# Sinkhorn attention and a bilinear FFN on one core: mixing k and v with tokens on partitions, up to three units ahead

## The chip, the cores and the metric

The kernel runs on one core of a Trainium2 chip. The metric is the device time of one execution in microseconds (us). "PE" is TensorE, "DVE" VectorE, "ACT" ScalarE, "POOL" GpSimd and "SP" SyncE, which here only issues DMAs.

## The reference, cut to what matters

```python
# batch 4, heads 8, sequence 768, head_dim 64; the sequence is cut into 8 blocks of 96
P = sort_net                                    # 8 x 8 for each head
for _ in range(5):                              # Sinkhorn: exp, then rows, then columns
    ...
k_sorted = einsum('bhij,bhjcd->bhicd', P, k_b)  # "mix": blocks of k weighted by P
v_sorted = einsum('bhij,bhjcd->bhicd', P, v_b)
scores   = q_b @ k_sorted.T / sqrt(64)          # 96 x 96 in each block
attn_out = softmax(scores) @ v_sorted
x        = attn_out as (3072, 512)
out      = ((x @ w_a) * (x @ w_b)) @ w_out      # 512 -> 1536 -> 512
```

## The kernel before

Heads are taken in pairs: four pairs make a batch, pairs 4 to 7 are batch 1, pairs 8 to 11 batch 2, and so on. The FFN of one batch and the attention of the next are interleaved on PE: after every few FFN steps stands one unit of attention work. `c` mixes k and v of a pair, `s` computes the scores and their exponential, `o` applies the weights to v and sends the result, by a DMA transpose, into `xT`, the left operand of the next batch's FFN.

```python
def stage_mix(g, what, engines):                # the mix, with head_dim on partitions
    src2 = loaded[g][0 if what == "k" else 1]   # 128 tokens x 2 heads x 384
    to = (kTs if what == "k" else vTs)[g % NBUF]
    mix = psA.tile([P, 2, 512], FP32, tag="A", name="mix")
    for c in range(NCH):                        # 6 chunks x 2 heads = 12 matmuls,
        for e in range(2):                      # weights 128x64, 128 columns each
            nc.tensor.matmul(mix[e * D:(e + 1) * D, c // 3, c % 3 * P:(c % 3 + 1) * P],
                             lhsT=src2[:, e, c * D:(c + 1) * D],
                             rhs=s_all[:, 2 * g + e], start=True, stop=True)
    ...                                         # evict to kT (ACT) or vT (half DVE, half ACT)
    if what == "v" and g > HP:                  # v must turn back: tokens on partitions
        nc.sync.dma_start_transpose(out=vss[g % NBUF][:, :, V0:V0 + P],
                                    in_=to.rearrange("p i t -> p (i t)"))

def to_xT(g):                                   # all of the FFN's x goes this way
    nc.sync.dma_start_transpose(out=xT[:, g % HP, :]..., in_=xp...)

def ffn_ab(b, m, t):                            # "pf": 8 matmuls of 384 columns, 4 for a, 4 for b
    ...                                         # ACT evicts a, DVE multiplies it with b into hT

def store(b, c, po):                            # one of six 128x512 pieces of a batch's output
    o_sb = ffp.tile([P, DMODEL], FP32, tag="o_sb", name="o_sb", bufs=3)
    copy("act" if c % 2 == 0 else "dve", o_sb, po)
    ...                                         # DMA to the output, from the SP queue

def c_(g):                                      # a unit of the interleaved attention
    ...
    stage_mix(g, "k", ("act",))
    stage_mix(g, "v", ("dve", "act"))
    if 2 * HP - 2 <= g < B * HP - 2:            # the gate holds the loads back on POOL
        nc.gpsimd.tensor_copy(out=gate, in_=kTs[g % NBUF][0:1, 0:1])
        load_pair((g + 2) // HP, (g + 2) % HP)
# units of a batch: c0 s0 c1 s1 c2 o0 s2 c3 o1 s3 o2 o3
```

The softmax here doesn't subtract the row's maximum and nothing guards it: scores larger than these inputs give would overflow.

Of the kernel before, what the change touches and what calls it, by code (L numbers as in the profile page):

```python
# [9 lines left out]
FP32 = mybir.dt.float32  # L10
BF16 = mybir.dt.bfloat16
# [11 lines left out]
def kernel(  # L23
# [11 lines left out]
    nc = tc.nc  # L35
    P = 128
    B, H, S, D = q.shape
    NB = sort_net.shape[-1]
    BLK = S // NB
# [6 lines left out]
    NCH = S // P  # L46
    HP = H // 2
    KA = DMODEL // P
    KO = DFF // P
# [5 lines left out]
    V0 = 16  # L55
    W = NCH * D
# [8 lines left out]
    att = ctx.enter_context(tc.tile_pool(name="att", bufs=4))  # L65
    ffp = ctx.enter_context(tc.tile_pool(name="ffp", bufs=2))
    psA = ctx.enter_context(tc.tile_pool(name="psA", bufs=2, space=PSUM))
# [18 lines left out]
    loaded = {}  # L86

    def load_pair(b, hp):
        tiles = []
        for name, t in (("k2", k), ("v2", v), ("q2", q)):  # L90
            base = (b * H + 2 * hp) * S * D
            if b == 0 and name == "q2":
                continue
            to = ld.tile([P, 2, W], BF16, tag=name, name=name)
            nc.gpsimd.dma_start(out=to, in_=_ap(t, base, [[W, P], [S * D, 2], [1, W]]))  # L95
            tiles.append(to)
        loaded[b * HP + hp] = tiles
# [27 lines left out]
    NBUF = 3  # L125
    kTs = [const.tile([P, S + PAD], BF16, name=f"kT{n}") for n in range(NBUF)]
    vTs = [const.tile([P, NB, P], BF16, name=f"vT{n}") for n in range(NBUF)]
    eTs = [const.tile([BLK, 2, 2, HB + PAD], BF16, name=f"eT{n}") for n in range(NBUF)]
    vss = [const.tile([P, NB, VW], BF16, name=f"vs{n}") for n in range(NBUF)]
# [11 lines left out]
    st = {}  # L141
# [7 lines left out]
    gate = const.tile([1, 1], BF16, name="gate")  # L149
    s_all = const.tile([P, BH, NB, CG], BF16, name="s_all")  # L150
# [9 lines left out]
    def copy(eng, out, in_):  # L160
        if eng == "act":
            nc.scalar.copy(out=out, in_=in_)  # L162
        else:
            nc.vector.tensor_copy(out=out, in_=in_)  # L164
# [79 lines left out]
    def pair_q(g):  # L244
        qc = qtp.tile([P, NCH, 2, D], BF16, tag="qc", name="qc", bufs=4)
        nc.gpsimd.tensor_copy(out=qc.rearrange("p c e d -> p e c d"),  # L246
                              in_=loaded[g][2].rearrange("p e (c d) -> p e c d", c=NCH))
        st[g, "qc"] = qc

    def stage_q(g):  # L250
        qT = qtp.tile([P, NCH, P], BF16, tag="qTf", name="qTf", bufs=4)
        nc.sync.dma_start_transpose(out=qT, in_=st[g, "qc"].rearrange("p c e d -> p (c e d)"))
        st[g, "qT"] = qT

    def turn_q(g, eng="dve"):
        q2 = loaded[g][2] if g >= HP else q_first[:, 2 * g:2 * g + 2]
        q_ps = psF.tile([P, NCH, P], BF16, tag="F", name="q_ps")
        for c in range(NCH):
            for e in range(2):
                nc.tensor.matmul(q_ps[e * D:(e + 1) * D, c, :],  # L260
                                 lhsT=q2[:, e, c * D:(c + 1) * D],
                                 rhs=ident, is_transpose=True)
        qT = qtp.tile([P, NCH, P], BF16, tag="qT", name="qT")
        copy(eng, qT, q_ps)
        st[g, "qT"] = qT

    def turn_v(g):
        vT, vs = vTs[g % NBUF], vss[g % NBUF]
        vs_ps = psF.tile([P, NB, P], BF16, tag="F", name="vs_ps")
        for i in range(NB):  # L270
            nc.tensor.matmul(vs_ps[:, i], lhsT=vT[:, i], rhs=ident, is_transpose=True)
        nc.vector.tensor_copy(out=vs[0:BLK, :, V0:V0 + P], in_=vs_ps[0:BLK])

    def stage_mix(g, what, engines):
        src2 = loaded[g][0 if what == "k" else 1]
        to = (kTs if what == "k" else vTs)[g % NBUF]
        pitch, whole = (BLK, S + PAD) if what == "k" else (P, NB * P)
        mix = psA.tile([P, 2, 512], FP32, tag="A", name="mix")
        for c in range(NCH):
            for e in range(2):  # L280
                nc.tensor.matmul(  # L281
                    mix[e * D:(e + 1) * D, c // 3, c % 3 * P:(c % 3 + 1) * P],
                    lhsT=src2[:, e, c * D:(c + 1) * D],
                    rhs=s_all[:, 2 * g + e], start=True, stop=True)
        for hf, eng in enumerate(engines):
            n = 2 // len(engines)
            for u in range(n):
                d1 = _ap(to, (hf + u) * 3 * CG, [[whole, P], [CG, 3], [pitch, NB], [1, CG]])
                s1 = _ap(mix, (hf + u) * 512, [[1024, P], [P, 3], [CG, NB], [1, CG]])
                copy(eng, d1, s1)  # L290
        if what == "v" and g > HP:
            nc.sync.dma_start_transpose(out=vss[g % NBUF][:, :, V0:V0 + P],
                                        in_=to.rearrange("p i t -> p (i t)"))

    def stage_scores(g):
        kT, qT, eT = kTs[g % NBUF], st[g, "qT"], eTs[g % NBUF]
        for hf in range(2):
            sc = psA.tile([P, 2, 512], FP32, tag="A", name="sc")
            for i in range(NBH):
                for e in range(2):  # L300
                    blk = hf * NBH + i
                    nc.tensor.matmul(  # L302
                        sc[:, e, i * BLK:(i + 1) * BLK],
                        lhsT=kT[e * D:(e + 1) * D, blk * BLK:blk * BLK + P],
                        rhs=qT[e * D:(e + 1) * D, :, blk * CG:(blk + 1) * CG],
                        start=True, stop=True)
            nc.scalar.activation(out=eT[:, hf, :, 0:HB], in_=sc[0:BLK, :, 0:HB],  # L307
                                 func=AF.Exp, scale=float(scale))

    def stage_o(g):  # L310
        xp = att.tile([BLK, NB, 2, D], BF16, tag="xp", name="xp")
        for hf in range(2):
            one_o(eTs[g % NBUF], hf, vss[g % NBUF], hf * NBH, xp, NB)
        st[g, "xp"] = xp

    def to_xT(g):
        xT, xp = xT_of(g // HP), st[g, "xp"]
        nc.sync.dma_start_transpose(
            out=xT[:, g % HP, :].rearrange("p (i t) -> p i t", i=NB),
            in_=xp.rearrange("p i e d -> p (i e d)"))  # L320


    hTs = {}
# [10 lines left out]

    def hT_of(b):
        if b not in hTs:
            hTs[b] = ffp.tile([P, KO, S], BF16, tag="hT", name="hT")
        return hTs[b]

    def ffn_ab(b, m, t, begun=()):  # L340
# [58 lines left out]
    with tc.manual_schedule(engines={ET.PE, ET.Pool, ET.SP}):  # L399
        with tc.manual_schedule(engines={ET.Activation, ET.DVE}):  # L400
# [7 lines left out]
            for it in range(5):  # L408
# [15 lines left out]
                if it > 0:  # L424
                    nc.tensor.matmul(heat[0:NB, 1, 0:NB], lhsT=rsum, rhs=rsum,
                                     start=True, stop=True)
# [103 lines left out]
            us.append(lambda: half_x(1, HP - 1, "dve"))  # L530
            return us

        def units_full(b):
            g0, us = b * HP, []

            def c_(g):
                if g < 2 * HP - 2:
                    turn_q(g)
                stage_mix(g, "k", ("act",))
                stage_mix(g, "v", ("dve", "act"))  # L540
                if 2 * HP - 2 <= g < B * HP - 2:
                    nc.gpsimd.tensor_copy(out=gate, in_=kTs[g % NBUF][0:1, 0:1])  # L542
                    load_pair((g + 2) // HP, (g + 2) % HP)

            def s_(g):
                stage_scores(g)
                if g == HP:
                    turn_v(g)
                if g in (HP, HP + 1):
                    stage_q(g + 2)  # L550
                if 2 * HP <= g + 1 < B * HP:
                    pair_q(g + 1)
                    stage_q(g + 1)

            def o_(g):
                stage_o(g)
                to_xT(g)

            for u, n in ((c_, 0), (s_, 0), (c_, 1), (s_, 1), (c_, 2), (o_, 0), (s_, 2), (c_, 3),
                         (o_, 1), (s_, 3), (o_, 2), (o_, 3)):  # L560
                us.append(lambda u=u, g=g0 + n: u(g))
            return us

        def interleave(steps, units, spare, slow=0):
            n, done = len(steps), 0
# [4 lines left out]
                    units[done]()  # L570
                    done += 1

        def paced(ab, po, units, spare):
            steps = ab + po
            total = len(steps) - 2 * spare
            done = 0
            for now, step in enumerate(steps, 1):
                step()
                while done < len(units) and done * total < now * len(units):
                    units[done]()  # L580
                    done += 1

        steps = [lambda: ffn_ab(0, 0, 0, begun[0:2]), lambda: ffn_ab(0, 1, 0, begun[2:4]),
                 lambda: ffn_ab(0, 2, 0, begun[4:5])]
# [3 lines left out]
        for b in range(B):  # L588
            ab = [lambda m=m, t=t, b=b: ffn_ab(b, m, t)
                  for m in range(KO) for t in range(2) if b > 0 or t == 1]  # L590
            po = [f for c in range(NCH) for f in ffn_out(b, c)]
            paced(ab, po, units_full(b + 1) if b + 1 < B else [], 3 if b == 0 else 2)


# [28 lines left out]
```

## Time and profile before

| | before |
|---|---|
| median of 3 executions | 245.35 us (245.03 to 245.57) |
| span of the profiled execution | 243.3 us |
| PE busy | 237.4 us, 98% |
| granted PE clock | 1.00 |

The first lines to read are on the page of the profile: busy time by engine with its share of the span, and the chain of work that ended last, by engine and by line.

```profile
...
PE 237.4 (98%) x2309; PEld 141.6 (58%) x2309; DVE 109.1 (45%) x258; ACT 104.4 (43%) x204; POOL 61.4 (25%) x88
...
PE 93%; DVE 4%; ACT 1%; DMA 1%; issue 0%
PE pf L332 52%; PE po L377 24%; PE mix L281 4%; PE o_ps L231 3%; PE sc L302 2%; PE mixh L180 2%; PE po L362 1%; PE vs_ps L208 1%; PE xt_ps L222 1%; PE sc L195 1%; DMA p_nat<-in_sort_net_dram 1%; PE heat L168 1%; PE two L332 1%; PE q_ps L260
...
```

PE is busy for 98% of the span, and the chain runs over PE for 93% of it, so the time is what PE must stream. The next view is the same chain in order of time (start us, length us, what), at the mixes of pairs 5 and 7.

```profile
...
51.00 0.46 PE q_ps L260 x12
51.46 0.67 PE mix L281 x24
52.13 1.41 PE pf L332 x8
...
63.83 0.79 PE mix L281 x24
64.62 1.41 PE pf L332 x8
...
```

A pair's two mixes are 24 matmuls in 0.79 us, or 0.67 us where the q turns (`q_ps`) come first. The eight projections (`pf`) behind them take 1.41 us; eight projections in the open take 1.30 us (2.60 us for 16, elsewhere in the same view). So a pair that stands between projections costs 0.12 us at the change to the small matmuls and 0.11 us at the change back, 0.90 us in all.

```profile
...
xT<-xp SPq DMA_TRANSPOSE x2, 2.8
```

The transpose of pair 7's `xT`, the last one that batch 1's FFN needs, is the second of the two issued from 75.43 us. It lands 2.8 us after its issue, by about 80 us, 4 us before PE asks for it. POOL's line for the first load of pair 10 (start us, us) is needed for the comparison below:

```profile
...
87.45 0.72 POOL L95 DMA_DIRECT2D k<-in_k_dram  x1 [0.34 <-issue]
...
```

### The profile page before, as it was taken

Reading aid. Unit: us, or ns where it says so; the run is one execution under the profiler, and the core shown is the slowest. Engines: PE = TensorE matmul, PEld = TensorE weight load, DVE = VectorE, ACT = ScalarE, POOL = GpSimd, SP = SyncE. Lnnn points to the kernel's source line nnn. Section 1 sums busy time; section 2 is a strip of 40 time slices with the busy share of each in tenths; the row PEclk is TensorE's granted clock in tenths of the full one; section 3 lists DMA queues with packets and bytes.
Section 4 is the critical chain, followed back from the end, with each engine's and each line's share of the span. In section 5 each row is a group of like instructions: output and inputs, shape, how many; then the busy total and the mean of one; then the engine's idle time right before and its main releaser. Section 6 shows DMA issues by size and latency. Waiting matters only on the chain.

```text
span 243.3 us, 5625 instructions
## 1 busy us (share of the span) xinstructions
PE 237.4 (98%) x2309; PEld 141.6 (58%) x2309; DVE 109.1 (45%) x258; ACT 104.4 (43%) x204; POOL 61.4 (25%) x88
## 2 busy tenths in 40 slices
PE   7999999999999999999999999999999999999994
PEld 7776666666554466666654466666654466665442
DVE  6774557555435234464534144363625144344110
ACT  3675853565630175736330165737330133333001
POOL 8766569623220053240400054200000000000000
PEclk9999999999999999999999999999999999999999
DMA  5999999985999589993964369923524310000132
GB/s 78 202 198 196 196 201 201 203 138 83 158 204 153 130 70 155 171 138 70 136 115 122 115 120 114 159 51 58 47 75 131 109 43 0 3 0 1 46 129 86
DMA packets 53930, 28.04 MB, mean 115 GB/s; under 512 B 30736, under 2 KB 50960, under 8 KB 53904
## 3 DMA queue, kind: packets, MB, share of 16 engines
q0 software_dynamic: 20944, 14.16, 41.6%
q1 hardware_dynamic: 32816, 13.45, 28.0%
q8 instruction: 18, 0.29, 0.5%
q14 instruction: 8, 0.07, 0.1%
q10 hardware_dynamic: 144, 0.07, 0.1%
HBM read 28.32 MB, written 6.29 MB: 142 GB/s over the span
## 4 chain that ended last, share of the span: by engine, by line
PE 93%; DVE 4%; ACT 1%; DMA 1%; issue 0%
PE pf L332 52%; PE po L377 24%; PE mix L281 4%; PE o_ps L231 3%; PE sc L302 2%; PE mixh L180 2%; PE po L362 1%; PE vs_ps L208 1%; PE xt_ps L222 1%; PE sc L195 1%; DMA p_nat<-in_sort_net_dram 1%; PE heat L168 1%; PE two L332 1%; PE q_ps L260 1%; DVE xp L237 1%
## 5 line engine op out<-in xcount | busy, mean ns | idle before, releaser
L353 DVE TENSOR_TENSOR hT<-a_sb,pf 128x384 bf16<-128x384 bf16 x95 | 52.6, 553 | 73.8 <-PE pf L332 46.4
L332 PE MATMUL pf<-xT,w_a_sb 128*128 128x384 bf16 x380 | 78.0, 326 | 0.2 <-ACT xT L162 0.2
L332 PE MATMUL pf<-xT,w_b_sb 128*128 128x384 bf16 x380 | 77.5, 326 | 0.0
L352 ACT CAST a_sb<-pf 128x384 bf16<-128x384 f32 x95 | 45.5, 479 | 60.9 <-PE pf L332 41.3
L377 PE MATMUL po<-w_out_sb,hT 128*128 128x512 bf16 x276 | 61.9, 379 | 0.0
L332 PEld LDWEIGHTS <-w_b_sb 128*128 128x128 bf16 x384 | 37.5, 98 | 24.8 <-issue 0.3
L332 PEld LDWEIGHTS <-w_a_sb 128*128 128x128 bf16 x384 | 34.9, 98 | 22.2
L377 PEld LDWEIGHTS <-hT 128*128 128x128 bf16 x276 | 26.3, 98 | 30.0
L162 ACT COPY o_sb<-po 128x512 f32<-128x512 f32 (+1 forms) x13 | 7.5, 577 | 46.8 <-PE po L377 45.2
L164 DVE COPY o_sb<-po 128x512 f32<-128x512 f32 (+1 forms) x12 | 7.9, 656 | 35.2 <-PE po L377 26.3
L307 ACT ACTIVATE eT<-sc 96x768 bf16<-96x768 f32 x24 | 18.0, 802 | 6.9 <-PE sc L302 6.9
L542 POOL COPY gate<-kT 1x1 bf16<-1x1 bf16 x8 | 1.4, 179 | 74.7 <-ACT kT L162 74.7
L237 DVE TENSOR_TENSOR xp<-o_ps,rec 96x512 bf16<-96x512 f32 x24 | 15.9, 684 | 0.6 <-DVE rec L235 0.2
L162 ACT CAST kT<-mix 128x384 bf16<-128x384 f32 x24 | 10.3, 482 | 8.0 <-PE mix L281 8.0
L95 POOL DMA_DIRECT2D k<-in_k_dram x16 | 11.6, 724 | 4.5 <-PE pf L332 2.3
L95 POOL DMA_DIRECT2D v<-in_v_dram x16 | 11.5, 721 | 3.1 <-DMA w_b_sb<-in_moe_w_b_dram 1.2
L231 PEld LDWEIGHTS <-eT 96*128 96x128 bf16 x256 | 10.4, 97 | 3.2 <-DVE xp L237 0.6
L235 DVE RECIPROCAL rec<-o_ps 96x8 f32<-96x8 f32 x32 | 5.6, 189 | 13.8 <-PE o_ps L231 13.8
L231 PE MATMUL o_ps<-vs,eT 96*128 96x65 bf16 x256 | 11.3, 193 | 0.2 <-DVE xp L237 0.2
L246 POOL COPY qc<-q 128x768 bf16<-128x768 bf16 x10 | 8.4, 842 | 7.2 <-DMA q<-in_q_dram 7.2
L95 POOL DMA_DIRECT2D q<-in_q_dram x12 | 8.7, 721 | 1.7 <-DMA w_a_sb<-in_moe_w_a_dram 0.7
L168 PE MATMUL heat<-warm 128*128 128x128 bf16 x84 | 7.6, 264 | 1.3 <-DVE warm L77 1.3
(80 smaller groups left out, 158.3 us busy)
## 6 DMA issues: line engine op xcount, KB each, us to landing
out_dram<-o_sb SPq DMA_DIRECT2D x17, 256.0 KB, 2.0
k<-in_k_dram POOLq DMA_DIRECT2D x16, 192.0 KB, 6.0
v<-in_v_dram POOLq DMA_DIRECT2D x16, 192.0 KB, 6.4
q<-in_q_dram POOLq DMA_DIRECT2D x12, 192.0 KB, 6.7
w_a_sb<-in_moe_w_a_dram POOLq DMA_DIRECT2D x6, 256.0 KB, 9.8
w_b_sb<-in_moe_w_b_dram POOLq DMA_DIRECT2D x6, 256.0 KB, 10.0
w_out_sb<-in_moe_w_out_dram POOLq DMA_DIRECT2D x3, 512.0 KB, 10.8
out_dram<-o_sb SPq DMA_DIRECT2D x12, 128.0 KB, 2.4
```

Source lines behind the costliest of these rows:

```text
L95: nc.gpsimd.dma_start(out=to, in_=_ap(t, base, [[W, P], [S * D, 2], [1, W]]))
L162: nc.scalar.copy(out=out, in_=in_)
L168: nc.tensor.matmul(ps[:, 0:cols], lhsT=warm[:, 0:P], rhs=warm[:, 0:cols], start=True, stop=True)
L231: nc.tensor.matmul(o_ps[:, e, i * (D + 1):(i + 1) * (D + 1)], lhsT=eT[:, hf, e, i * BLK:i * BLK + P], rhs=vs[0:BLK, i0 + i, V0 - 1 + e * ( ...
L237: nc.vector.tensor_tensor(out=_ap(xp, i0 * 2 * D, [[nxp * 2 * D, BLK], [D, 2], [2 * D, NBH], [1, D]]), in0=_ap(o_ps, 1, [[1024, BLK], [511 ...
L246: nc.gpsimd.tensor_copy(out=qc.rearrange("p c e d -> p e c d"), in_=loaded[g][2].rearrange("p e (c d) -> p e c d", c=NCH))
L281: nc.tensor.matmul(mix[e * D:(e + 1) * D, c // 3, c % 3 * P:(c % 3 + 1) * P], lhsT=src2[:, e, c * D:(c + 1) * D], rhs=s_all[:, 2 * g + e], ...
L307: nc.scalar.activation(out=eT[:, hf, :, 0:HB], in_=sc[0:BLK, :, 0:HB], func=AF.Exp, scale=float(scale))
L332: nc.tensor.matmul(pf[:, 0:HW], lhsT=w_sb[:, kc, m * P:(m + 1) * P], rhs=x_cols(b, kc, t), start=(kc == 0), stop=(kc == KA - 1))
L352: nc.scalar.copy(out=a_sb, in_=pf[:, 0:HW])
L353: nc.vector.tensor_mul(out=hT[:, m, t * HW:(t + 1) * HW], in0=a_sb, in1=ab[1][:, 0:HW])
L377: nc.tensor.matmul(held["po"], lhsT=hTs[b][:, m, c * P:(c + 1) * P], rhs=w_out_sb[:, m, :], start=(m == 0), stop=(m == KO - 1))
```

## The change

The intent is to take work off PE. For k of pairs 5 to 15 and v of pairs 8 to 15 the operands of the mix are swapped: the mixing matrix becomes the weight and the tokens come out on partitions, in 2 matmuls of 384 columns instead of 12 of 128. The result then lies the wrong way round for the scores, so each such mix needs a DMA transpose from SP, and a copy on POOL that puts the tokens in block order. For v a second transpose follows, as before. To hide this the mixes run up to three units ahead: batch 2's first two pairs are now mixed in the phase of batch 0's FFN. One hT buffer is given up.

```diff
+    def stage_plain(g, what, engines):
+        mix = psA.tile([P, 2, 512], FP32, tag="A", name="mix")
+        for e in range(2):
+            nc.tensor.matmul(mix[:, e, 0:W], lhsT=s_all[:, 2 * g + e], rhs=src2[:, e], ...)
+        nat = att.tile([P, NCH, 2, D], BF16, tag="nat", name="nat")
+        ...                                                  # evict mix to nat
+        nc.sync.dma_start_transpose(out=turned, in_=nat...)
+        st[g, what] = turned
+    def in_order(g, what):
+        nc.gpsimd.tensor_copy(out=to, in_=st[g, what]...)    # turned to kT or vT
+    def return_v(g):
+        nc.sync.dma_start_transpose(out=vss[g % NBUF]..., in_=vTs[g % NBUF]...)
...
-                if 2 * HP - 2 <= g < B * HP - 2:
-                    nc.gpsimd.tensor_copy(out=gate, in_=kTs[g % NBUF][0:1, 0:1])
-                    load_pair((g + 2) // HP, (g + 2) % HP)
...
+        plan(0, "c4", "c5", "s4", "c6", "s5", "o4", "c7", "s6", "o5", "c8", "s7", "o6", "o7", "c9")
+        plan(1, "s8", "c10", "s9", "o8", "c11", "s10", "o9", "c12", "s11", "o10", "o11", "c13")
+        plan(2, "s12", "c14", "s13", "o12", "c15", "s14", "o13", "s15", "o14", "o15")
+        after = [[] for _ in seq]
+        for n, (b, u, g) in enumerate(seq):
+            if u is c_ and g > HP:
+                for what in "kv":
+                    if plain(g, what):
+                        after[n + 1].append(lambda g=g, what=what: in_order(g, what))
+                after[n + 3 if g % HP == 0 else n + 1].append(lambda g=g: load_later(g))
+                if plain(g, "v"):
+                    after[n + 2].append(lambda g=g: return_v(g))
...
-            hTs[b] = ffp.tile([P, KO, S], BF16, tag="hT", name="hT")
+            hTs[b] = ffp.tile([P, KO, S], BF16, tag="hT", name="hT", bufs=1)
```

The functions in `after[n]` run when unit n has been issued. On POOL, therefore, the loads of pair g+2 stand behind the reorder copies of pair g.

More of the change, by code (lines that the diff above doesn't have):

```diff
@@ L290, in stage_mix, with plain, stage @@
                 copy(eng, d1, s1)
-        if what == "v" and g > HP:
-            nc.sync.dma_start_transpose(out=vss[g % NBUF][:, :, V0:V0 + P],
-                                        in_=to.rearrange("p i t -> p (i t)"))
+    def plain(g, what):
+        return g >= (2 * HP if what == "v" else HP + 1)
+    def stage_plain(g, what, engines):
+        src2 = loaded[g][0 if what == "k" else 1]
+        mix = psA.tile([P, 2, 512], FP32, tag="A", name="mix")
+        for e in range(2):
+            nc.tensor.matmul(mix[:, e, 0:W], lhsT=s_all[:, 2 * g + e], rhs=src2[:, e],
+                             start=True, stop=True)
+        nat = att.tile([P, NCH, 2, D], BF16, tag="nat", name="nat")
+        step = 2 // len(engines)
+        for u, eng in enumerate(engines):
+            copy(eng, nat[:, :, u * step:(u + 1) * step].rearrange("p c e d -> p e c d"),
+                 mix[:, u * step:(u + 1) * step, 0:W].rearrange("p e (c d) -> p e c d", c=NCH))
+        turned = att.tile([P, NCH, P], BF16, tag="turned", name="turned")
+        nc.sync.dma_start_transpose(out=turned, in_=nat.rearrange("p c e d -> p (c e d)"))
+        st[g, what] = turned
+    def stage(g, what, engines):
+        (stage_plain if plain(g, what) else stage_mix)(g, what, engines)
+    def in_order(g, what):
+        if what == "k":
+            to = kTs[g % NBUF][:, 0:S].rearrange("p (i c t) -> p c i t", i=NB, c=NCH)
+        else:
+            to = vTs[g % NBUF][:, :, 0:BLK].rearrange("p i (c t) -> p c i t", c=NCH)
+        nc.gpsimd.tensor_copy(out=to, in_=st[g, what].rearrange("p c (i t) -> p c i t", i=NB))
+    def return_v(g):
+        nc.sync.dma_start_transpose(out=vss[g % NBUF][:, :, V0:V0 + P],
+                                    in_=vTs[g % NBUF].rearrange("p i t -> p (i t)"))
     def stage_scores(g):
@@ L531, in units_half, with c_ @@
             return us
-        def units_full(b):
-            g0, us = b * HP, []
-            def c_(g):
-                if g < 2 * HP - 2:
-                    turn_q(g)
-                stage_mix(g, "k", ("act",))
-                stage_mix(g, "v", ("dve", "act"))
-                if 2 * HP - 2 <= g < B * HP - 2:
-                    nc.gpsimd.tensor_copy(out=gate, in_=kTs[g % NBUF][0:1, 0:1])
-                    load_pair((g + 2) // HP, (g + 2) % HP)
-            def s_(g):
-                stage_scores(g)
-                if g == HP:
-                    turn_v(g)
-                if g in (HP, HP + 1):
-                    stage_q(g + 2)
-                if 2 * HP <= g + 1 < B * HP:
-                    pair_q(g + 1)
-                    stage_q(g + 1)
-            def o_(g):
-                stage_o(g)
-                to_xT(g)
-            for u, n in ((c_, 0), (s_, 0), (c_, 1), (s_, 1), (c_, 2), (o_, 0), (s_, 2), (c_, 3),
-                         (o_, 1), (s_, 3), (o_, 2), (o_, 3)):
-                us.append(lambda u=u, g=g0 + n: u(g))
-            return us
+        def c_(g):
+            stage(g, "k", ("act",))
+            stage(g, "v", ("dve", "act"))
+            if HP < g < 2 * HP:
+                return_v(g)
+            if g >= 2 * HP:
+                pair_q(g)
+                stage_q(g)
@@ new lines, in s_, with o_, load_later, plan @@
+        def s_(g):
+            stage_scores(g)
+            if g == HP:
+                turn_v(g)
+            if g in (HP, HP + 1):
+                stage_q(g + 2)
+        def o_(g):
+            stage_o(g)
+            to_xT(g)
+        def load_later(g):
+            if 2 * HP - 2 <= g < B * HP - 2:
+                load_pair((g + 2) // HP, (g + 2) % HP)
+        units = [[] for _ in range(B)]
+        seq = []
+        def plan(b, *names):
+            for name in names:
+                seq.append((b, {"c": c_, "s": s_, "o": o_}[name[0]], int(name[1:])))
@@ L564, in interleave, with unit @@
+        def unit(u, g, then):
+            if u is c_ and g < 2 * HP - 2:
+                turn_q(g)
+            u(g)
+            for f in then:
+                f()
+        for (b, u, g), then in zip(seq, after):
+            units[b].append(lambda u=u, g=g, then=then: unit(u, g, then))
         def interleave(steps, units, spare, slow=0):
@@ L571, in interleave, with paced @@
                     done += 1
-        def paced(ab, po, units, spare):
+        def paced(ab, po, units, spare, last):
             steps = ab + po
             total = len(steps) - 2 * spare
-            done = 0
+            main, done = len(units) - last, 0
             for now, step in enumerate(steps, 1):
                 step()
-                while done < len(units) and done * total < now * len(units):
+                while done < main and done * total < now * main:
                     units[done]()
                     done += 1
+                if now == len(steps) - 1 and last:
+                    units[main]()
         steps = [lambda: ffn_ab(0, 0, 0, begun[0:2]), lambda: ffn_ab(0, 1, 0, begun[2:4]),
@@ L591 @@
             po = [f for c in range(NCH) for f in ffn_out(b, c)]
-            paced(ab, po, units_full(b + 1) if b + 1 < B else [], 3 if b == 0 else 2)
+            paced(ab, po, units[b], 3 if b == 0 else 2, 1 if b < B - 2 else 0)
 _INS = ['q', 'k', 'v', 'sort_net', 'moe_w_a', 'moe_w_b', 'moe_w_out']
```

## The prediction

> **Bound now.** TensorE (PE). The busy table gives PE 237.4 of 243.3 us (98%), VectorE 45%, ScalarE 43%, GpSimd 25%; the chain of waits is 93% PE; in stretches of 4 us PE is full from 28 to 236 us but for 0.2 us near 74. So after 28 us the time is the sum of what PE streams. 77% of the chain is projections, untouched.
>
> **PE work.** 19 of 24 mixes (k of pairs 5 to 15, v of pairs 8 to 15) go from 12 matmuls (128x64 weights, 128 columns) to 2 (128x128, 384 columns). In the chain a k+v pair takes 0.79 us, and the 8 pf matmuls after it 1.41 instead of 1.30: 0.90 us. The old matmuls already overlap in twos (28 ns each), so little is halved: at pf's 1.30/8 = 0.163 us the new pair is estimated at 4 x 0.163 = 0.65 us. The 0.11 us fits the Trainium skill, "TensorEngine Tiling (Array Packing)", Key Properties: changing the tiling mode drains TensorE.
> - Pairs 8 to 15: 8 x 0.25 = 2.0 us saved.
> - Pairs 6, 7 (plain k, tiled v): 0.
> - Pair 5 (tiled q turns, plain k, tiled v): two switches more, 0.2 us lost.
> Net -1.8 us.
>
> **Added elsewhere.** Evictions stay (two kT casts of 0.43 become one of about 0.8). 19 DMA transposes on the SP queue, 1.2 us of issue each; the like qTf transposes landed in 2.8 us on idle DMA engines, 9.9 behind the weight loads. 19 GpSimd reorder copies, estimated by the qc copy at 0.84 us: 16 us on a quarter-busy engine. One hT buffer costs nothing: PE runs the phases in order anyway.
>
> **Critical path.** It matters only where a mix or reorder comes late. Between mix and scores now lie eviction 0.8, transpose 3 to 6, reorder 0.9. From pair 8 on the plan gives over 10 us. Batch 1 is tight: pair 5 is mixed at 47.4; its transpose, issued at 49, lands at about 54 (weight loads fill the DMA engines until 52.5); reordered by 55; scores due at 56. Pair 8's loads follow pair 6's reorder on GpSimd, start at 59 to 60, land (4.0 to 6.6 us in the trace) at 64 to 67; their mix is due at 68, not 85. I count 0.3 us of expected stall, with a tail of 2 to 4.
>
> **Predicted: 243.9 us** (245.35 - 1.8 + 0.3), range 243.0 to 246.5; faster by over 2% 0.03, within 2% 0.92, slower by over 2% 0.05.
>
> **Right or wrong in the profile.**
> - 190 fewer matmuls; plain mixes stream in 0.16 us each; pf after them 1.30, not 1.41.
> - The first FFN phase (44 to 84 us), which takes over two pairs of mixes, grows by about 1.5 us; the next (54.5 us) shrinks by 1.0, the third (54.5 us) by 2.3; the last (from 193 us) keeps its length.
> - PE full after 28 us; new idle time would stand at 55 to 70 us, before pair 5's or 6's scores (released by GpSimd) or pair 8's mix (released by a load).
> - DMA busy rises by 19 x about 1.2 us; batch 0's stores go out later, without holding PE.
>
> **What would make it wrong.** A stall over 2 us at pair 5, 6 or 8; reorder copies (runs of 16 elements) far slower than 0.84 us, holding the loads behind them; SP's in-order queue held by a transpose that waits for GpSimd, so that xT or stores come late; switches that cost more than I read, which would save more.

## More of the kernel before

Windows of 4 us, with the busy time of PE, weight loads, DVE, ACT and POOL, then the granted clock, the DMA engines' mean load and GB/s. They cover the boundary between batch 0's FFN and batch 1's (84.2 us).

```profile
...
84.00:88.00 4.00, 4.00 (x45) 2.48 (x44) 2.02 (x4) 2.20 (x5) 0.73 (x2) 1.00 0.46 105
88.00:92.00 4.00, 4.00 (x39) 2.38 (x38) 1.45 (x3) 2.79 (x5) 2.44 (x4) 1.00 1.26 53
...
```

PE has no gap at the boundary. The operand that makes it possible is `xT`. Two views show how it comes: the SP queue's instructions (start us, us, queue, line, operation), and the landing time of DMAs that were being issued from 76 to 80 us (the last number is us from issue to landing, a median where there are several).

```profile
...
75.43 2.61 SPq L318 DMA_TRANSPOSE xT<-xp  x2
78.14 7.95 SPq L390 DMA_DIRECT2D out_dram<-o_sb  x8
...
```

Finally the DMA queue of the whole run that carries SP's transposes and stores (packets, MB, share of 16 engines' span).

```profile
...
q1 hardware_dynamic: 32816, 13.45, 28.0%
...
```

## The result, and the profile after

| | before | after |
|---|---|---|
| median | 245.19 us (4 executions) | 247.94 us (4 executions, 247.24 to 248.63) |
| span of the profiled execution | 243.3 us | 245.8 us |
| PE busy | 237.4 us | 236.2 us |
| PE idle at the phase boundary | none | 2.79 us |
| granted PE clock, mean | 1.00 | 0.993 |

The ratio is 1.011, with a 95% interval of 1.0075 to 1.0145. Ratios here are the mean time of one kernel's runs over that of the other's of the same rounds, so they are not quite the ratios of the medians quoted. The kernel became slower, by about 1%, where about 0.6% of gain was forecast.

First the same lines of the page as before.

```profile
...
PE 236.2 (96%) x2109; PEld 139.2 (57%) x2119; DVE 109.0 (44%) x258; ACT 104.2 (42%) x193; POOL 75.0 (31%) x99
...
PE 82%; DMA 9%; DVE 4%; POOL 2%; ACT 1%; SPq 1%; issue 1%; POOLq 0%; DVEq 0%
PE pf L361 49%; PE po L406 18%; DMA out_dram<-o_sb 3%; DMA xT<-xp 3%; DMA turned<-nat 3%; PE o_ps L231 3%; PE mix L299 2%; PE sc L331 2%; PE mixh L180 2%; PE po L391 1%; PE vs_ps L208 1%; PE mix L281 1%; PE xt_ps L222 1%; PE sc L195 1%; DMA
...
```

PE's share of the chain fell from 93% to 82%, and DMA took 9%. Now the chain in order of time at pair 5 (four lines) and pair 10 (two).

```profile
...
47.28 0.46 PE q_ps L260 x12
47.74 0.43 PE mix L299 x2
48.17 0.46 PE mix L281 x12
48.63 1.41 PE pf L361 x8
...
94.52 0.65 PE mix L299 x4
95.17 3.90 PE pf L361 x24
...
```

The forecast of the PE work holds line by line. A pair with both mixes in the new form takes 0.65 us, and the 24 projections after it 3.90 us, with nothing lost at the switch; before, it was 0.79 + 0.11. That is 0.25 us less. The chain shows it so for pairs 10, 11, 12, 14 and 15; the same is assumed for pairs 8, 9 and 13, which are mixed among `po` matmuls in the new order, where the kernel before has no like place. Pair 6, in the same view, takes 0.33 + 0.46 + 1.41 = 2.20 us, as the old pair did. Pair 5 takes 0.46 + 0.43 + 0.46 + 1.41 = 2.76 us against 0.46 + 0.67 + 1.41 = 2.54 us before.

The time went at the boundary between two FFN phases. PE's own instructions there (start us, busy us, line, operation, and in brackets the idle time before it and what ended it):

```profile
...
84.09 1.46 PE L406 MATMUL po<-w_out_sb,hT 128*128 128x512 bf16 x6
85.39 0.65 PE L361 MATMUL pf<-xT,w_a_sb 128*128 128x384 bf16 x3
88.83 0.32 PE L361 MATMUL pf<-xT,w_a_sb 128*128 128x384 bf16 x1 [2.79 <-DMA xT<-xp]
...
```

PE ran the three matmuls of its first projection that need pairs 4 to 6 and then stood 2.79 us for pair 7's `xT`. Windows of 1 us show what followed.

```profile
...
89.00:90.00 1.00, 1.00 (x11) 0.48 (x11) 0.54 (x1) 0.48 (x1) 0.00 (x0) 0.80 1.07 377
90.00:91.00 1.00, 1.00 (x18) 0.69 (x15) 0.62 (x2) 0.65 (x1) 0.00 (x0) 0.50 1.26 233
91.00:92.00 1.00, 1.00 (x5) 0.47 (x4) 0.00 (x0) 0.86 (x2) 0.37 (x1) 0.50 1.24 263
92.00:93.00 1.00, 1.00 (x5) 0.46 (x3) 0.00 (x0) 0.48 (x1) 1.00 (x2) 0.50 0.70 138
93.00:94.00 1.00, 1.00 (x7) 0.59 (x6) 0.55 (x1) 0.03 (x1) 1.00 (x3) 0.99 0.86 203
...
```

PE resumed at 88.83 us, but from about 89.6 to 93.0 us the granted clock was a half. Against a full clock, the column PEclk loses 0.20 + 0.50 + 0.50 + 0.50 + 0.01 = 1.71 us of work. A like drop followed PE's gap in the two other traced runs that have one near this place (e1 and e9 below); in the other seven traces the clock was 1.00 from 28 to 236 us. So 2.79 + 1.71 = 4.50 us were lost, 8 x 0.25 - 0.22 = 1.8 us were gained in the mixes and 0.12 us by an earlier start of the phases, which leaves 2.6 us; the span grew by 2.5 us.

Why was `xT` late? SP's queue at the boundary, and the landing of what was being issued from 81.8 to 83.2 us:

```profile
...
76.85 1.71 SPq L347 DMA_TRANSPOSE xT<-xp  x1
80.18 1.56 SPq L321 DMA_TRANSPOSE vs<-vT  x1
81.83 1.35 SPq L347 DMA_TRANSPOSE xT<-xp  x1
...
```

```profile
...
v<-in_v_dram POOLq DMA_DIRECT2D x1, 192.0 KB, 5.2
q<-in_q_dram POOLq DMA_DIRECT2D x1, 192.0 KB, 6.7
xT<-xp SPq DMA_TRANSPOSE x1, 7.0
```

Two things happened to the transpose of pair 7's `xT` (81.83 us). Its data was ready at 77.04 us (the end of DVE's last `xp`, 76.35 + 0.69 in DVE's timeline), and SP was free at 78.56, but the return of pair 8's v stood first in SP's program, and SP sat until 80.18 us before issuing that. Then, instead of landing in 2.8 us, `xT` took 7.0 us, beside loads of v and q. That these loads are to blame for the 7.0 us is so far only argued; e5 below tests it. POOL shows where both came from:

```profile
...
68.70 0.82 POOL L318 COPY kT<-turned 128x768 bf16<-128x768 bf16 x1 [8.01 <-DMA turned<-nat]
69.46 0.72 POOL L95 DMA_DIRECT2D k<-in_k_dram  x1
...
79.33 0.83 POOL L318 COPY vT<-turned 128x768 bf16<-128x768 bf16 x1 [0.89 <-DMA turned<-nat]
80.10 0.72 POOL L95 DMA_DIRECT2D k<-in_k_dram  x1
...
81.90 0.72 POOL L95 DMA_DIRECT2D q<-in_q_dram  x1
...
```

The reorder copy of pair 7's k (68.70) waited 8.01 us for its transpose. Behind it in POOL's program stood pair 9's loads (69.46). Pair 8's two transposes, issued from 69.54 us beside these loads, took 7.9 us (k) and 8.3 us (v) to land; the prediction had reckoned with 3 to 6 us. The view of what was being issued from 70.8 to 72.2 us has the line for v:

```profile
...
turned<-nat SPq DMA_TRANSPOSE x1, 8.3
...
```

So the reorder of pair 8's v came only at 79.33, which released the return on SP, and behind it pair 10's loads went out at 80.10 to 82.62 us. In the kernel before, pair 10's loads went out from 87.45 us, after the boundary (line above). The reorder copy itself takes 0.83 us, as forecast.

The same queue's line shows the added volume: it went from 28.0% of 243.3 us to 37.4% of 245.8 us, that is from 68 to 92 us, 24 us more; 19 x 1.2 = 23 us had been forecast. The match may be luck: the only 1.2 us in the prediction is SP's time to issue a transpose, which is not the time that its packets take on the DMA engines.

```profile
...
q1 hardware_dynamic: 48016, 17.19, 37.4%
...
```

The queue of POOL's loads took another 41.7%, so over the whole run the DMA engines still had room. It was the meeting at 80 to 89 us that hurt.

### The profile page after: what moved, and what is told of

It is laid out like the page before. It is cut to its first block, busy times and chain, and to the rows that moved or that the text cites. A ratio compares the mean times of both kernels' runs of the same rounds, so it can differ in the third digit from the quotient of the medians.

```text
span 245.8 us, 5281 instructions
## 1 busy us (share of the span) xinstructions
PE 236.2 (96%) x2109; PEld 139.2 (57%) x2119; DVE 109.0 (44%) x258; ACT 104.2 (42%) x193; POOL 75.0 (31%) x99
## 3 DMA queue, kind: packets, MB, share of 16 engines
q0 software_dynamic: 20944, 14.16, 41.7%
q1 hardware_dynamic: 48016, 17.19, 37.4%
## 4 chain that ended last, share of the span: by engine, by line
PE 82%; DMA 9%; DVE 4%; POOL 2%; ACT 1%; SPq 1%; issue 1%; POOLq 0%; DVEq 0%
PE pf L361 49%; PE po L406 18%; DMA out_dram<-o_sb 3%; DMA xT<-xp 3%; DMA turned<-nat 3%; PE o_ps L231 3%; PE mix L299 2%; PE sc L331 2%; PE mixh L180 2%; PE po L391 1%; PE vs_ps L208 1%; PE mix L281 1%; PE xt_ps L222 1%; PE sc L195 1%; DMA p_nat<-in_sort_net_dram 1%
## 5 line engine op out<-in xcount | busy, mean ns | idle before, releaser
L361 PE MATMUL pf<-xT,w_a_sb 128*128 128x384 bf16 x380 | 78.8, 328 | 3.0 <-DMA xT<-xp 2.8
L406 PE MATMUL po<-w_out_sb,hT 128*128 128x512 bf16 x266 | 60.7, 379 | 0.5
L361 PEld LDWEIGHTS <-w_a_sb 128*128 128x128 bf16 x384 | 35.7, 98 | 22.9 <-issue 0.5
L318 POOL COPY kT<-turned 128x768 bf16<-128x768 bf16 x11 | 9.1, 829 | 77.0 <-DMA turned<-nat 64.6
L162 ACT CAST nat<-mix 128x768 bf16<-128x768 f32 (+1 forms) x19 | 12.6, 664 | 9.4 <-PE mix L299 8.2
L168 PE MATMUL heat<-warm 128*128 128x128 bf16 x84 | 7.0, 250 | 1.3 <-DVE warm L77 1.3
```

Source lines behind the costliest of these rows:

```text
L162: nc.scalar.copy(out=out, in_=in_)
L318: nc.gpsimd.tensor_copy(out=to, in_=st[g, what].rearrange("p c (i t) -> p c i t", i=NB))
L361: nc.tensor.matmul(pf[:, 0:HW], lhsT=w_sb[:, kc, m * P:(m + 1) * P], rhs=x_cols(b, kc, t), start=(kc == 0), stop=(kc == KA - 1))
L406: nc.tensor.matmul(held["po"], lhsT=hTs[b][:, m, c * P:(c + 1) * P], rhs=w_out_sb[:, m, :], start=(m == 0), stop=(m == KO - 1))
```

## The experiments

Two theories stood at the start. A: SP's in-order queue held `xT` behind the return. B: the DMA engines were too busy, and `xT` was slow in flight. A rival for both was that the new mixes themselves cost more than thought (C); the 0.65 us and 3.90 us above speak against C, and the runs below that reach 243 us with all 19 new mixes in place (e5, e8, e12) rule it out. All eight kernels gave correct results.

| run | edit to the changed kernel | median us (lowest to highest) | ratio to before, 95% interval |
|---|---|---|---|
| e1 | return of pair 8 behind `xT` of pair 7 | 245.35 (244.16 to 247.11) | 1.0011 (0.9974 to 1.0049) |
| e5 | pair 10's loads after `xT` of pair 7 | 243.45 (243.04 to 243.91) | 0.9927 (0.9911 to 0.9944) |
| e4 | order alone, all mixes tiled | 245.09 (244.88 to 246.40) | 0.9994 (0.9980 to 1.0009) |
| e7 | batch 1's k tiled | 243.12 (242.98 to 243.72) | 0.9916 (0.9902 to 0.9930) |
| e8 | e1 and six output buffers | 243.21 (243.09 to 244.56) | 0.9936 (0.9918 to 0.9955) |
| e9 | six output buffers alone | 248.95 (247.68 to 250.45) | 1.0160 (1.0127 to 1.0192) |
| e12 | loads of pairs 8 and 9 before the reorders | 243.11 (242.93 to 243.81) | 0.9925 (0.9911 to 0.9938) |
| e13 | e7, e1 and six output buffers | 243.04 (242.94 to 243.09) | 0.9916 (0.9903 to 0.9928) |

The first four ran on one chip (before: 245.15 us median of 11), the last four on another (before: 245.04 us median of 11).

### e1: the return behind xT

```diff
-                    after[n + 2].append(lambda g=g: return_v(g))
+                    after[n + (3 if g == 2 * HP else 2)].append(lambda g=g: return_v(g))
```

> Edit: only the return transpose of v of pair 8 moves behind xT of pair 7 in SP's program order; all else as in the changed kernel. Theory A (SP's in-order queue): xT of pair 7 had its data at 77.0 us but stood behind that return, which waited for GpSimd's reorder until 80.2, so it was issued at 81.8. Now it is issued at about 78.6 and lands by 82 to 85, before the 86.0 us at which PE needs it: no idle PE there, no drop of the clock; 2.8 us idle and 1.7 us of lost clock go, median about 243.4. Theory B (the DMA engines are simply full of 19 more transposes, with loads and stores): xT still takes about 7 us and every transfer only changes places; PE still idles over 1 us near 86, median 245.5 or more. Theory C (the new mixes cost PE more than thought): PE busy without idle and still over 245.

The median was 245.35 us, between the theories. PE got `xT` in time; that part of A held. But in the profiled execution, the slowest of the six (247.11 us), PE stood 2.29 us a little later. PE's instructions, then DVE's:

```profile
...
87.21 0.82 PE L361 MATMUL pf<-xT,w_a_sb 128*128 128x384 bf16 x4
90.32 1.05 PE L361 MATMUL pf<-xT,w_b_sb 128*128 128x384 bf16 x4 [2.29 <-DVE o_sb L164]
...
```

```profile
...
89.58 0.69 DVE L164 COPY o_sb<-po 128x512 f32<-128x512 f32 x1 [4.75 <-DMA out_dram<-o_sb]
...
```

DVE waited 4.75 us for a store of batch 0's output to land and free one of three output buffers. The copy empties `po`, and `po` and the projections `pf` take turns in the same four PSUM buffers (tag "F" in the kernel). PE's next projection was due for a buffer of that pool, and PE went on at 90.32 us, 0.05 us after the copy had ended (89.58 + 0.69). In the changed kernel the same copy waited nearly as long:

```profile
...
89.46 0.69 DVE L164 COPY o_sb<-po 128x512 f32<-128x512 f32 x1 [4.61 <-DMA out_dram<-o_sb]
...
```

There PE was already waiting for `xT`, so this second wait lay hidden under the first. A's forecast of 243.4 us failed by this second wait, in the execution that was traced. The six executions spread over 3 us, and the three fastest (244.16 to 244.90, clock 0.999 to 1.0) are still about 1 us above e8's; how long the wait was in them is not known, since they weren't traced.

### e8 and e9: six output buffers, with and without e1

```diff
-            o_sb = ffp.tile([P, 512], FP32, tag="o_sb", name="o_sb", bufs=3)
+            o_sb = ffp.tile([P, 512], FP32, tag="o_sb", name="o_sb", bufs=6)
...
-        o_sb = ffp.tile([P, DMODEL], FP32, tag="o_sb", name="o_sb", bufs=3)
+        o_sb = ffp.tile([P, DMODEL], FP32, tag="o_sb", name="o_sb", bufs=6)
```

> Edit: the return behind xT as in the run before (e1), and six output buffers in place of three. In that run PE got its xT in time but stood 2.3 us later, at 88 to 90.3: VectorE waited with the last output copy of batch 0 until a store of batch 0 had landed and freed its buffer (89.6), and behind it no projection was evicted. Theory A2 (that wait is a second one, caused by stores that go out late, and nothing else is left): with free buffers VectorE never waits for a store, PE has no gap near 88, every run has the clock at 1.0, median about 243.4. If PE still idles over 0.5 us between 84 and 96, or the median is over 244.3, there is a third wait or the contention itself holds PE.

The median was 243.21 us; no copy waited for a store in the trace, and PE was full from 84 to 96 us. One execution of 244.56 us stands apart, with the clock at 1.0; its cause is open, since it wasn't the profiled one.

> Edit: the changed kernel with six output buffers in place of three, and SP's order untouched. Theory A2: xT of pair 7 still stands behind the return of pair 8, is issued at 81 to 82 and lands at 87 to 89; PE idles 1.5 to 3 us before it and the clock falls; median 246.5 to 248. If instead the buffers were the root (late copies making late stores making a late xT): xT in time, about 243.5.

The median was 248.95 us, worse than the changed kernel and above the forecast of 246.5 to 248. The wait for `xT` was 4.41 us in the profiled execution:

```profile
...
90.37 0.48 PE L361 MATMUL pf<-xT,w_a_sb 128*128 128x384 bf16 x1 [4.41 <-DMA xT<-xp]
...
```

So the buffers were not the root: `xT` was late though no copy waited for a buffer. It was issued at 81.44 us, 0.4 us earlier than in the changed kernel, but its landing, from the view of what was being issued from 81.4 to 82.8 us, took 8.9 us instead of 7.0:

```profile
...
xT<-xp SPq DMA_TRANSPOSE x1, 8.9
...
```

Why it took longer still is not shown. This run also clears up the chain on the changed kernel's page, which puts a store before that transpose (`DMA out_dram<-o_sb` 3%): here, without any wait for a store, `xT` was issued at the same place behind the return. With SP's order changed alone (e1) the store wait is left, and with the buffers alone (e9) the wait for `xT`; e8 has neither. The runs that move the loads (e5, e7, e12) need no more buffers: in their traces the last output copy of batch 0 doesn't wait for a store, so the store wait goes with the traffic at the boundary too.

### e5: pair 10's loads only after xT

```diff
             if 2 * HP - 2 <= g < B * HP - 2:
+                if g == 2 * HP:
+                    nc.gpsimd.tensor_copy(out=gate, in_=xTs[1][0:1, HP - 1, 0:1])
                 load_pair((g + 2) // HP, (g + 2) % HP)
...
-        plan(1, "s8", "c10", "s9", "o8", ...
+        plan(1, "s8", "o8", "c10", "s9", ...
```

> Edit: SP's order stays as in the changed kernel, but the loads of pair 10 wait on GpSimd until xT of pair 7 has landed; the mix of pair 10 comes one unit later to make up for it. Theory B (contention): xT of pair 7, issued at 81.8 as before, lands in 3 to 4 us instead of 6.95, at about 85 to 86: PE idles under 0.5 us, median about 243.5 to 244. Theory A alone (only the place in the queue counts): it still takes 6 us or more, PE idles over 2 us, median about 247.5.

The landing of `xT` of pair 7 (issued at 81.74 us), and POOL's gate with the first load behind it:

```profile
...
xT<-xp SPq DMA_TRANSPOSE x1, 3.0
```

```profile
...
84.78 0.18 POOL L585 COPY gate<-xT 1x1 bf16<-1x1 bf16 x1 [4.69 <-DMA xT<-xp]
85.02 0.72 POOL L95 DMA_DIRECT2D k<-in_k_dram  x1
...
```

SP's order was untouched up to this transpose (the edit also moves the mix of pair 10, and with it its transposes, behind `o8`, which comes later), and the transpose was issued 0.09 us earlier than in the changed kernel. It landed in 3.0 us instead of 7.0, PE never waited, and the median was 243.45 us. This is theory B in a narrow form: not the 19 transposes as such, which were all there, but the loads that came in the same few microseconds. That agrees with the Trainium skill, "DMA: Bandwidth & Descriptors", Queues, rings and completion order: each DMA engine goes round its queues packet by packet. The traces give 7.0 us beside the loads and 3.0 us without them; the order of the packets was not looked at. A transpose on SP's queue must share with loads on POOL's queue, though it was issued from another engine.

### e4: the order alone

```diff
     def plain(g, what):
-        return g >= (2 * HP if what == "v" else HP + 1)
+        return False
...
-            if HP < g < 2 * HP:
+            if g > HP:
                 return_v(g)
...
             if 2 * HP - 2 <= g < B * HP - 2:
+                nc.gpsimd.tensor_copy(out=gate, in_=kTs[g % NBUF][0:1, 0:1])
                 load_pair((g + 2) // HP, (g + 2) % HP)
```

> Edit: every mix in the old tiled form, with the units in the changed kernel's order and one hT buffer (a small GpSimd copy that reads kT releases the loads, as in the kernel before). Without the new transposes xT of pair 7 should be issued at about 78.5 and land by 82. If the order costs nothing by itself: median 245.2 within 0.5, no idle PE near 86, PE work as in the kernel before. If looking ahead is itself what collides: idle PE near 86 and over 246.5.

The median was 245.09 us. Running ahead neither costs nor gains by itself, and one hT buffer costs nothing that shows. One limit: without reorder copies POOL issued pair 10's loads at 70.8 us here, so this run doesn't have the collision either. The traced execution is the slowest (246.40 us): its first projection started at 22.07 us, against 21.08 in the kernel before, behind a late load of k, so about 1.0 us of its excess arose before anything that this edit touches.

### e7 and e12: two ways to start the loads earlier

e7 keeps k of pairs 5 to 7 in the old form, and gates the loads of pairs 8 and 9 on kT as the kernel before did.

```diff
     def plain(g, what):
-        return g >= (2 * HP if what == "v" else HP + 1)
+        return g >= 2 * HP
...
+                if g < 2 * HP:
+                    nc.gpsimd.tensor_copy(out=gate, in_=kTs[g % NBUF][0:1, 0:1])
                 load_pair((g + 2) // HP, (g + 2) % HP)
```

> Edit: k of pairs 5 to 7 goes back to the tiled form (three transposes and three reorder copies fewer, before pair 8 is mixed); batches 2 and 3 and SP's order as in the changed kernel. PE work falls by the 0.2 us of switches at pair 5. Theory A/B as a chain (pair 7's late reorder delays pair 9's loads, these delay pair 8's transposes, these hold the return and with it xT): the return of pair 8 is released by about 76 to 77 instead of 80.2, xT of pair 7 is issued by 79 and lands before 86: median about 243.2. If instead the return still holds xT to 81 or later: 246 to 248.

The median was 243.12 us. The transpose of pair 7's `xT` was issued at 79.71 us, a little later than forecast, and was in time. But e7 changes two things: three transposes are gone, and the loads no longer stand behind a reorder. e12 separates them, by keeping all 19 transposes and moving only the loads.

```diff
+                if g in (2 * HP - 2, 2 * HP - 1):
+                    def first(g=g):
+                        nc.gpsimd.tensor_copy(out=gate, in_=st[g, "k", "nat"][0:1, 0, 0, 0:1])
+                        load_later(g)
+                    after[n].append(first)          # ahead of in_order(g) on POOL
                 for what in "kv":
                     if plain(g, what):
                         after[n + 1].append(lambda g=g, what=what: in_order(g, what))
-                after[n + 3 if g % HP == 0 else n + 1].append(lambda g=g: load_later(g))
+                if g not in (2 * HP - 2, 2 * HP - 1):
+                    after[n + 3 if g % HP == 0 else n + 1].append(lambda g=g: load_later(g))
```

> Edit: the changed kernel, but on GpSimd the loads of pairs 8 and 9 stand before the reorder copies of pairs 6 and 7 and are released by the eviction of that pair's k; all 19 transposes and reorders stay, and SP's order too. Theory D (the late loads are the start of the chain): loads of pair 9 are issued at 62 to 63 instead of 69.5 and no longer meet the transposes of pair 8, whose v is reordered by 77 instead of 80.2; xT of pair 7 lands before 86, loads of pair 10 are done earlier as well; median about 243.5. Theory B2 (the volume of 19 transposes is what counts, wherever the loads stand): PE idles over 1 us between 84 and 92; median over 245.

The median was 243.11 us, like e7's. POOL's lines for pair 9's first load, the reorder of pair 8's v, and pair 10's first load, and then the landing of `xT` of pair 7:

```profile
...
62.59 0.71 POOL L95 DMA_DIRECT2D k<-in_k_dram  x1 [0.28 <-issue]
...
73.87 0.83 POOL L319 COPY vT<-turned 128x768 bf16<-128x768 bf16 x1
74.64 0.72 POOL L95 DMA_DIRECT2D k<-in_k_dram  x1
...
```

```profile
...
xT<-xp SPq DMA_TRANSPOSE x1, 3.9
```

Pair 9's loads began at 62.59 us instead of 69.46, the reorder of pair 8's v at 73.87 instead of 79.33, and pair 10's loads at 74.64 instead of 80.10, so that they were nearly through when `xT` went out. That transpose was issued at 80.81 us, only 1.0 us earlier than in the changed kernel, because the issue of the one before it took SP 3.18 us; it landed in 3.9 us and was in time. So theory D of the recorded text held: with the volume unchanged, the place of the loads on POOL decides.

### e13: e7, e1 and six output buffers together

This is e7 with the edits of e1 and of the six buffers. The recorded text calls the late loads left out, but e7's own edit had already moved pair 9's loads to 62.18 us, much as e12 does (62.59).

> Edit: batch 1's k tiled as in e7, the return of pair 8 behind xT of pair 7, six output buffers: every cure at once except for the late loads. If e7 has no wait left on PE, nothing is to be gained: median 243.1 within 0.25, the same PE busy time as e7 within 0.3 us. If e7 still loses something to late stores or xT: under 242.8.

The median was 243.04 us, the same as e7 within 0.1 us (on another chip; the ratio to the kernel before is 0.9916 for both). Nothing that these waits cost is left on PE. e7, e8, e12 and e13 all lie between 243.04 and 243.21 us, about 2 us below the kernel before, so they beat both kernels, as e5 does with 243.45. e7's and e13's executions are the closest together.

## Why the prediction was wrong

- **The bound and the PE work: right.** PE work was forecast to fall by 1.8 us (2.0 less 0.2 at pair 5). The chain shows 0.25 us for each of the five pairs from 10 on that can be compared, 0 at pair 6 and 0.22 us lost at pair 5. Without waits the gain is 245.04 - 243.11 = 1.93 us in e12's medians. The 0.2 us at pair 5, seen in the chain, is too small to be told from e7's and e12's times.
- **Phases: right where no wait came in.** The second FFN phase began at 85.39 us instead of 84.17, and the phases began 0.12 us earlier overall (42.15 for 42.27 us), so the first grew by 1.34 us (1.5 forecast). The third shrank from 54.52 to 52.24 us, by 2.3 as forecast, and the last kept its length. The second was to shrink by 1.0 us but grew from 54.52 to 58.21 us: that is the forecast missed by 4.7 us, of which 4.5 us are the wait and the clock.
- **The step that failed: "I count 0.3 us of expected stall, with a tail of 2 to 4", placed at 55 to 70 us, and "batch 0's stores go out later, without holding PE".** There was no stall before pair 5's or 6's scores or pair 8's mix. The stall was at the boundary at 86 us, for `xT`: 2.79 us idle and 1.71 us of halved clock. The prediction named the mechanism among what would make it wrong ("SP's in-order queue held by a transpose that waits for GpSimd, so that xT or stores come late"), but gave it no cost. What it mis-sized on that way was the transpose itself: "transpose 3 to 6", where pair 7's k took 6.6 us and pair 8's k and v 7.9 and 8.3 us. It counted the way of every new operand from mix to scores, and not what the new transfers do to an old one. `xT` had 4 us to spare before; the queue took 3.3 us of it (78.56 to 81.83) and the shared DMA engines 4.2 us (7.0 instead of 2.8).
- **It followed the moved loads only as far as pair 8.** It had pair 8's loads follow pair 6's reorder, but didn't ask where that puts the loads of pairs 9 and 10. Pair 10's loads went from 87.45 us, after the boundary, to 80.10 us, on top of the last `xT` and the stores.
- **The stores did hold PE once `xT` came in time by a new order alone** (e1): a store held a DVE copy, and the copy held the PSUM buffer that PE needed. e8 shows it by taking that wait away.
- **The drop of the clock was not counted at all.** It made a 2.8 us wait cost 4.5 us.

What stays open: which part the queue and which part the shared engines had in a single execution can't be split exactly, since either cure brings `xT` in time. e5 shows that taking the contention away, with SP's order kept, is enough; e1 shows that a better place in SP's queue brings `xT` in time too, but not the stores: the two `xT` transposes in flight from 77 to 82 us there still landed only after 6.2 us (median).

## What to carry to other kernels

When work leaves the bounding engine for DMA queues, list the transfers that were already there with little slack (here the last operand of the next phase, and the stores that must land before a copy can free a PSUM buffer), and ask what the new transfers and the moved loads do to them. Don't put a load's issue behind a copy that waits for another DMA on the same queue of instructions: the two issue orders of e12 and the changed kernel differ by nearly 5 us of 248 with the same work (243.11 and 247.94 us, on different chips; ratios to before 0.9925 and 1.011). After curing a wait, look for the next one below it before calling the theory wrong, and count a stall of PE with the clock that it loses.

## What the Trainium skill lacked or had wrong

- "TensorE: Matmul & The Clock Gate", Part 1, has PE fall back to half clock after at least one idle window of about 3.4 us. Here a gap of 2.79 us was followed by half clock, and in e1 one of 2.29 us. In the changed kernel the drop came about 0.8 us after PE had resumed, and lasted from about 89.6 to 93.0 us, which does fit the page's 3.4 us for the way back. In e1 it lasted from about 90.8 to 94.2 us, and in e9, after a gap of 4.41 us, from about 90.4 to 93.8 us.
- "DMA: Bandwidth & Descriptors", DMA Transpose (X-bar), gives constraints but, on the chip used here, no time for a transpose from SBUF to SBUF (a table elsewhere on the page, for trn3 B0, has the sequencer's cycles on unnamed previous generations, without the transfer). Measured for 128x768 bf16: SP is occupied 1.21 to 3.47 us for one issue (median 1.28), and it lands after 2.8 us where the engines were idle at its issue (54.82 us), up to 8.3 us beside loads and stores.
- "TensorEngine Tiling (Array Packing)", Key Properties, says that a change of tiling mode drains TensorE, but gives no cost. The chain agrees with it and gives one: 0.12 us into the tiled mixes (0.79 against 0.67 us where tiled q turns stood before them) and 0.11 us out of them (1.41 against 1.30 us for the projections). That is 0.23 of the 0.25 us gained at each pair: the mixes' own matmuls take 0.67 us in the old form and 0.65 us in the new one.
